# Attention and an expert layer in one kernel: where the preparation of w_out stands in the program

## The chip, the cores and the metric

The kernel runs on one core of a Trainium2 chip. The metric is device time in microseconds (us) of one execution. The core has five engines that run side by side and wait for one another by semaphores: TensorE (PE in the rows, with PEld for its weight loads), VectorE (DVE), ScalarE (ACT), GpSimd (POOL) and SyncE (SP), whose queue issues the DMAs here. Each engine takes its instructions strictly in the order in which the program lists them, so that an instruction that waits also holds back all that stand behind it on the same engine.

## The reference

```python
def _attn_ref(q, k, v):                      # 8 batches, 8 heads, 576 positions, 64 wide
    scores = scale * np.matmul(q, k.transpose(0, 1, 3, 2))
    mask = block_i >= block_j                # blocks of 64 positions
    scores = np.where(mask, scores, -1000000000.0)
    scores = scores - np.max(scores, axis=-1, keepdims=True)
    attn = np.exp(scores)
    attn = attn / (np.sum(attn, axis=-1, keepdims=True) + 1e-09)
    return np.matmul(attn, v)

def _moe_ref(x, w_in, w_out):                # 4608 tokens, 512 -> 2048 -> 512
    h = x @ w_in
    r = np.maximum(h, 0.0)
    return ((r * r) @ w_out)
```

The output of the attention, with the heads side by side, is the `x` of the second function. Everything is fp32 outside.

## The kernel before

**Attention** is worked in 40 passes, numbered 0 to 39. Passes 0 to 7 take the first 192 positions of batches 0 and 1, one pair of heads each; passes 8 to 15 take the other 384 positions of the same two batches; passes 16 to 39 take a whole pair of heads of batches 2 to 7. A pass is done in two or three groups of rows. For a group TensorE makes the scores (tile `ps`), VectorE the row maxima (`nmx`), ScalarE the exponentials with their sums (`sm`), VectorE the reciprocals (`rs`), and the probabilities (`p_rows`) are turned: in passes 8 to 11 by TensorE transposes (`pt`) that VectorE and ScalarE copy back, from pass 12 on by DMA transposes that SyncE issues (L480). Then TensorE multiplies by the values (`px`).

**The expert layer** is worked in 12 chunks of 384 tokens. A chunk's input (`xt`) is the normalized attention output as two fp16 parts. The hidden stage (`moe_in`) has 16 blocks of 12 matmuls (`ph`), each followed by ScalarE (`r`, `g`), GpSimd (`r*r`) and a subtraction (`g`, L680). The output stage (`moe_out`) has three accumulations of 48 matmuls (`po`), so a chunk has 192 + 144 = 336 matmuls. Chunk 0 holds what passes 0 to 7 give.

**The weights** come as fp32 in raw 64-bit blocks and are split into two fp16 parts on the core. `weight_scale(0)` and `weight_parts(0)` do it for w_in; `weight_scale(1)` and `weight_parts(1)` for w_out. For w_out each of the 16 blocks is loaded twice: once as `wa` for its maximum (VectorE, L245), once as `wb` for its parts: ScalarE `wt` (L283), three VectorE operations (L284, L287, L290), a ScalarE cast to `w2h` (L291), a GpSimd subtraction to `w2l` (L292). The scale of all parts needs the maxima of all 16 blocks; it goes through a transposition and a small matmul on TensorE (`pm_w`, L177 and L183). Both loads use the same ring of three buffers (`qk32`), which later holds the raw q and k of passes 16 on.

**What sets the order.** The Python program emits instructions in some order; that order is the priority. A scheduler then walks through them with a built-in timing and writes down for each engine the ready instruction of highest priority. The expert layer and the weights are generators, listed in `todo`; `fill(n)` advances them by n steps, and `pour` calls it between the groups of each pass (`FILL` gives the steps per pass). `first_moe` is the generator of chunk 0: a step is one block of the hidden stage or one block of w_in's parts; from the ninth block of the hidden stage on, each block is followed by one maximum of w_out, and when the hidden stage is through come the other maxima and then w_out's 16 blocks of parts, one a step. With 14 steps per pass, passes 8 to 11 take all of this in among their own work.

The constants `SC0`, `SCN`, `PTN` and `PT0` say where `first_moe` starts what; `WT`, `BP`, `BS`, `gate` and `behind` are switches for variants that are off.

Of the kernel before, what the change touches and what calls it, by code (L numbers as in the profile page):

```python
# [8 lines left out]
F32 = mybir.dt.float32  # L9
# [5 lines left out]
ALU = mybir.AluOpType  # L15
AX = mybir.AxisListType
PSUM = bass.MemoryType.PSUM

P = 128
# [5 lines left out]
NF = 16  # L25
# [6 lines left out]
A_X = 13  # L32
# [5 lines left out]

TLS = True
PRE = 0  # L40
SC0 = 8
SCN = 1
PTN = 3
PT0 = 16
G_POOL = 8
G_CK = 1
X_POOL = 1
QF = (6, 7)
WT = 1
IVN = 6  # L50
PT_MM = 8
EV = ((1, 1), (1, 0))
# [3 lines left out]
N_POOL = 0  # L56
N_HP = 2
NQ_CK = 1
BP = 99
BS = 99  # L60
NQ_POOL = 0
SQ_HP = 1
NG = 4
# [37 lines left out]
def attention_moe_kernel(ctx: ExitStack, tc: tile.TileContext, qkt, qk, vm, vt, w_in, w_out, out):  # L101
    nc = tc.nc
# [3 lines left out]
    p1 = ctx.enter_context(tc.tile_pool(name="p1", bufs=1))  # L106
# [98 lines left out]
        nc.sync.dma_start(raw, src[f])  # L205
        return words(raw)

    def behind(later, earlier):

        tc.add_manual_dep(  # L210
            later.ins,
            earlier.ins.name,
            mybir.DependencyInfo(mybir.DependencyClass.NoSync, mybir.DependencyReason.DATA),
            reason="order of use",
        )

    w1raw = []
    gate = {}

    wsc = [const.tile([P, n], F32, name=f"wsc{i}") for i, n in enumerate((NG, 1))]  # L220
    wm = const.tile([P, NG], F32, name="wm")
# [14 lines left out]
    def weight_scale(wi):  # L236

        tok, ng = ((tokA, NG), (tokB, 1))[wi]  # L240
        st = small.tile([P, NF], F32, tag="stw", name=f"stw_{wi}", bufs=1)
        n = NF // ng
        for f in range(NF):
            _, _, hf = load_w(w_out, f, f"wa{wi}_{f}") if wi else w1raw[f]
            i = nc.vector.tensor_reduce(st[:, f : f + 1], hf, axis=AX.X, op=ALU.max, apply_absolute_value=True)  # L245
            if wi == 0 and f >= BS and (1, 0) in gate:
                behind(i, gate[1, 0])
            if f % n == n - 1:
                q = f // n
                st1 = small.tile([P, 1], F32, tag="st1", name=f"st1_{wi}_{q}", bufs=1)  # L250
                nc.vector.reduce_max(st1, st[:, f + 1 - n : f + 1], axis=AX.X)
                m = pow2_of_max(st1, 1, f"w{wi}_{q}", 2.0**-27, wm[:, q : q + 1] if wi == 0 else None)
                s = wsc[wi][:, q : q + 1]
                nc.vector.tensor_scalar(
                    s.bitcast(I32), m.bitcast(I32), -1, (127 + W_TOP) << 23, op0=ALU.mult, op1=ALU.add
                )
            yield
        if wi == 0:
            m = small.tile([P, 1], F32, tag="m", name="m_w")
            nc.vector.reduce_max(m, wm, axis=AX.X)  # L260
        nc.vector.tensor_scalar(
            tok.bitcast(I32), m.bitcast(I32), 8, (127 - W_EXP) << 23, op0=ALU.mult, op1=ALU.add
        )
        if wi == 0:
            nc.vector.tensor_scalar(tokA, tokA, 2.0 ** (A_X + A_W - 1), None, op0=ALU.mult)
            inv = scale_of(m, 0, 1, "w")
            nc.vector.tensor_scalar(wm, wm, inv, None, op0=ALU.mult)
            nc.vector.tensor_tensor(wm, wm, wm, op=ALU.mult)
        else:
            nc.vector.tensor_scalar(tokB, tokB, tokA, None, op0=ALU.mult)  # L270
            nc.vector.tensor_scalar(wm, wm, wsc[1], None, op0=ALU.mult)

    def weight_parts(wi):

        wh, wl = ((w1h, w1l), (w2h, w2l))[wi]
        for f in range(NF):
            wlo, whi, hf = load_w(w_out, f, f"wb{wi}_{f}") if wi else w1raw[f]
            if WT:
                t = p1.tile([P, 512], F32, tag=("qs", "k1", "k2")[(wi + f) % 3], name=f"wt{wi}_{f}")
            else:  # L280
                t = p2.tile([P, 512], F32, tag="r", name=f"wt{wi}_{f}", bufs=3)
            q = f * NG // NF
            nc.scalar.activation(t, hf, AF.Copy, scale=(wm if wi else wsc[0])[:, q : q + 1])  # L283
            i = nc.vector.tensor_scalar(whi, whi, -(2**31), None, op0=ALU.bitwise_and)  # L284
            if wi == 0 and f >= BP and (1, 0) in gate:
                behind(i, gate[1, 0])
            nc.vector.scalar_tensor_tensor(  # L287
                whi, t.bitcast(I32), 3, whi, op0=ALU.logical_shift_left, op1=ALU.bitwise_or
            )
            nc.vector.scalar_tensor_tensor(whi, wlo, 29, whi, op0=ALU.logical_shift_right, op1=ALU.bitwise_or)  # L290
            nc.scalar.copy(wh[:, f], hf)  # L291
            nc.gpsimd.tensor_tensor(wl[:, f], hf, wh[:, f], op=ALU.subtract)  # L292
            yield
# [266 lines left out]
    def normalize(b, g):  # L560

        u = f"{b}_{g}"
        ck, o = place(b, g)
        w = D * TILES[g]
        if ck not in xts:
            slot = min(ck % 3, 1)
            xts[ck] = p1.tile([P, 2, NHP, CH], F16, tag=f"xt{slot}", name=f"xt_{ck}")
            ivs[ck] = small.tile([P, 3], F32, tag="iv", name=f"ivs_{ck}")
        x = x_of(b, g)
        early = ck < X_POOL  # L570
        nq = ps_x.tile([P, 512], F32, tag="x", name=f"nq_{u}")[:, :w]
        n = 3 * NHP // TILES[g]
        for a in range(0, NHP, n):
            sq = p1.tile([P, n, w], BF16, tag="sq", name=f"sq_{u}_{a}")
            if ck == 0 and SQ_HP:
                for hp in range(n):
                    nc.scalar.activation(sq[:, hp], x[:, a + hp], AF.Square)
            else:
                nc.scalar.activation(sq, x[:, a : a + n], AF.Square)
            k = n  # L580
            if ck >= NQ_CK:
                k = n // 2
                eng = nc.gpsimd if NQ_POOL else nc.vector
                eng.tensor_tensor(sq[:, 0:k], sq[:, 0:k], sq[:, k:n], op=ALU.add)  # L584
                if k > 1:
                    k = 1
                    eng.tensor_tensor(sq[:, 0:k], sq[:, 0:k], sq[:, k : 2 * k], op=ALU.add)
            for i in range(k):
                nc.tensor.matmul(nq, ones_bf, sq[:, i], start=(a + i == 0), stop=(a + n == NHP and i == k - 1))
        hb = p2.tile([P, CH], F32, tag="hb", name=f"hb_{u}")[:, :w]  # L590
        hi = hb.bitcast(I32)
        nc.vector.tensor_scalar(
            hi, nq.bitcast(I32), 1, EXPMASK, op0=ALU.logical_shift_right, op1=ALU.bitwise_and
        )
        gate[b, g] = nc.vector.tensor_scalar(hi, hi, -1, (190 + A_X) << 23, op0=ALU.mult, op1=ALU.add)  # L595
        xh, xl = xts[ck][:, 0, :, o : o + w], xts[ck][:, 1, :, o : o + w]
        if ck == 0 and b in N_DVE:
            for a in range(0, NHP, N_HP):
                hps = slice(a, a + N_HP)
                nc.vector.tensor_tensor(x[:, hps], x[:, hps], hb[:, None, :].to_broadcast([P, N_HP, w]), op=ALU.mult)  # L600
                (nc.scalar.copy if N_ACT else nc.vector.tensor_copy)(xh[:, hps], x[:, hps])
                (nc.gpsimd if N_POOL else nc.vector).tensor_tensor(xl[:, hps], x[:, hps], xh[:, hps], op=ALU.subtract)
            return ck, o, w, hb
        nc.gpsimd.tensor_tensor(x, x, hb[:, None, :].to_broadcast([P, NHP, w]), op=ALU.mult)  # L604
        (nc.scalar.copy if early else nc.vector.tensor_copy)(xh, x)  # L605
        nc.gpsimd.tensor_tensor(xl, x, xh, op=ALU.subtract)  # L606
        return ck, o, w, hb
# [22 lines left out]

    def first_moe(ck, firsts):

        scale, parts = weight_scale(1), weight_parts(1)
        hidden = moe_in(ck)
        n = 0
        while True:
            try:
                next(hidden)
            except StopIteration as e:
                gs = e.value  # L640
                break
            if n == IVN:
                for r in firsts:
                    inverses(*r)
            yield
            if next(parts0, 0) is None:
                yield
            for _ in range(SCN if n >= SC0 else 0):
                if next(scale, 0) is None:
                    yield  # L650
            if n == PT0:
                yield from scale
            for _ in range(PTN if n >= PT0 else 0):
                if next(parts, 0) is None:
                    yield
            n += 1
        for gen in (scale, parts):
            yield from gen
        yield from moe_out(ck, gs)

    def moe_in(ck):
# [116 lines left out]
    def emit(i0, i1):  # L778
        for i in range(i0, i1):
            one_pass(i, passes[i])  # L780
# [69 lines left out]
    todo.append(first_moe(0, firsts))  # L850
    front(passes[NT * NHP])
    pg = ctx.enter_context(tc.tile_pool(name="pg", bufs=16, reuse_waits="tile"))
    emit(NT * NHP, len(passes))
    while todo or waiting:
        fill(1)
# [32 lines left out]
```

## Time and profile before

| | us |
|---|---|
| median of 3 runs | 1152.78 (1150.38 to 1157.13) |
| the profiled execution | 1157.18 |
| its span, first to last instruction | 1155.4 |
| TensorE busy | 1035.3 (90%) |
| VectorE busy | 763.9 (66%) |
| ScalarE busy | 629.6 (54%) |
| GpSimd busy | 341.0 (30%) |

The busy time of TensorE is near to the span, so what the span has beyond it is the time in which TensorE waited. The table does not say where; the rows by stage below do. The mean granted clock over the span is 0.963 of the full one.

### The profile page before, as it was taken

What the parts mean: (1) busy time and instruction counts of PE and PEld (TensorE: products, weight loads), DVE (VectorE), ACT (ScalarE), POOL (GpSimd) and SP (SyncE); (2) the same over time, 40 slices, a digit from 0 to 9 for tenths busy, and PEclk for the clock granted to TensorE, in tenths of its full rate; (3) what the DMA queues carried; (4) which work ended last, traced back from release to release, by engine and by line L of the source; (5) the groups of instructions that cost most, each with busy time, mean ns of one, the idle gap of its engine ahead of it and who ended that gap; (6) DMA issues with size and microseconds to landing.
All of it is one profiled execution on the core that took longest, in us unless ns stands there. A gap on an engine that the chain in (4) does not pass through costs nothing. (4 is left out here: it accounts for less than half of the span.)

```text
span 1155.4 us, 18711 instructions
## 1 busy us (share of the span) xinstructions
PE 1035.3 (90%) x6836; PEld 541.6 (47%) x6836; DVE 763.9 (66%) x1783; ACT 629.6 (54%) x1492; POOL 341.0 (30%) x312
## 2 busy tenths in 40 slices
PE   6679777898989989899997999889889999999998
PEld 4234322354445445445544545445445545555453
DVE  6998789869778978868749857976896613212120
ACT  6586765557468548726737627726865723223140
POOL 2575145124112412422205302520340314312030
PEclk9799998899999999999999999989999999999999
DMA  8555177867687688855954657567848330000000
GB/s 282 194 186 194 56 193 188 198 140 140 144 165 156 114 191 164 155 115 114 186 120 84 141 111 138 119 140 148 170 80 169 48 78 20 10 19 1 28 1 28
DMA packets 337948, 142.25 MB, mean 123 GB/s; under 512 B 309696, under 2 KB 323008, under 8 KB 337856
## 3 DMA queue, kind: packets, MB, share of 16 engines
q1 hardware_dynamic: 337856, 141.06, 55.2%
q8 instruction: 53, 0.87, 0.3%
q14 instruction: 39, 0.32, 0.1%
HBM read 55.31 MB, written 9.44 MB: 56 GB/s over the span
## 5 line engine op out<-in xcount | busy, mean ns | idle before, releaser
L670 PE MATMUL ph<-xt,w1h 128*128 128x384 f16 x1536 | 381.2, 330 | 21.7 <-ACT r L676 10.4
L695 PE MATMUL po<-w2h,g 128*128 128x512 f16 x1152 | 359.7, 386 | 8.5 <-ACT w2h L291 8.5
L679 POOL TENSOR_TENSOR r<-r 128x384 f32<-128x384 f32 x192 | 178.6, 936 | 556.4 <-ACT g L678 520.3
L695 PEld LDWEIGHTS <-g 128*128 128x128 f16 x1728 | 166.3, 99 | 219.4 <-issue 34.1
L670 PE MATMUL ph<-xt,w1l 128*128 128x384 f16 x768 | 253.3, 330 | 0.0
L695 PE MATMUL po<-w2l,g 128*128 128x512 f16 x576 | 222.1, 386 | 4.2 <-POOL w2l L292 4.2
L670 PEld LDWEIGHTS <-w1h 128*128 128x128 f16 x1536 | 145.0, 99 | 129.6 <-issue 34.4
L452 ACT ACTIVATE p<-ps,nmx,es 128x320 f32<-128x320 f32 (+8 forms) x216 | 131.1, 616 | 135.9 <-DVE nmx L449 111.4
L676 ACT ACTIVATE r<-ph 128x384 f32<-128x384 f32 x192 | 93.2, 491 | 160.3 <-PE ph L670 147.9
L680 DVE TENSOR_TENSOR g<-r,g 128x384 f16<-128x384 f32 x184 | 113.7, 623 | 86.3 <-POOL r L679 86.2
L476 DVE SCALAR_TENSOR_TENSOR p_rows<-p,rs,p_rows 128x320 f16<-128x320 f32 (+8 forms) x240 | 143.5, 632 | 18.6 <-ACT p_rows L475 18.3
L475 ACT ACTIVATE p_rows<-p,rs 128x320 f16<-128x320 f32 (+8 forms) x240 | 120.3, 569 | 47.1 <-DVE rs L461 23.1
L446 DVE TENSOR_REDUCE nmx<-ps 128x1 f32<-128x192 f32 (+8 forms) x288 | 124.6, 479 | 23.5 <-PE ps L422 14.8
L678 ACT ACTIVATE g<-r 128x384 f16<-128x384 f32 x192 | 99.4, 525 | 4.0 <-POOL w1l L292 0.8
L670 PEld LDWEIGHTS <-w1l 128*128 128x128 f16 x768 | 75.8, 99 | 51.2 <-issue 2.2
L422 PE MATMUL ps<-kT,qT 128*64 128x64 f16 (+6 forms) x960 | 84.7, 297 | 10.6 <-DMA qT<-qs 5.8
L534 PE MATMUL px<-p_turned,v 128*64 128x384 f16 (+5 forms) x1168 | 79.3, 282 | 14.5 <-DMA p_turned<-p_rows 10.1
L702 DVE TENSOR_SCALAR ob<-po,uv 128x512 f32<-128x512 f32 x36 | 28.9, 805 | 95.7 <-PE po L695 95.7
L534 PEld LDWEIGHTS <-v 128*64 128x64 f16 x1128 | 54.7, 115 | 48.1 <-issue 22.1
L604 POOL TENSOR_TENSOR x<-x,hb 128x768 f32<-128x768 f32 (+1 forms) x16 | 44.6, 2785 | 94.9 <-DVE hb L595 92.8
L422 PEld LDWEIGHTS <-qT 128*64 128x64 f16 x960 | 45.9, 111 | 50.5 <-issue 31.7
L606 POOL TENSOR_TENSOR xt<-x,xt 128x768 f16<-128x768 f32 (+1 forms) x16 | 51.7, 3229 | 30.9 <-DVE xt L605 24.3
(129 smaller groups left out, 965.3 us busy)
## 6 DMA issues: line engine op xcount, KB each, us to landing
qk<-in_qk SPq DMA_DIRECT2D x24, 576.0 KB, 4.5
wa<-in_w_out SPq DMA_DIRECT2D x16, 512.0 KB, 4.3
wb<-in_w_out SPq DMA_DIRECT2D x16, 512.0 KB, 4.4
out<-ob SPq DMA_DIRECT2D x32, 256.0 KB, 2.1
vraw<-in_vm SPq DMA_DIRECT2D x30, 256.0 KB, 3.5
w1raw<-in_w_in SPq DMA_DIRECT2D x8, 512.0 KB, 6.6
kf<-in_qkt SPq DMA_DIRECT2D x8, 288.0 KB, 3.6
w2h<-in_w_in SPq DMA_DIRECT2D x4, 512.0 KB, 10.9
```

Source lines behind the costliest of these rows:

```text
L422: nc.tensor.matmul(ps[hs, o].rearrange("p (n d) -> p n d", d=D), t["qT"][:, j, hs], t["kT"][:, z, c0:c1, hs], start=(z == 0), stop=(z == 1),)
L446: nc.vector.tensor_reduce(nmx[:, i : i + 1], ps[:, off : off + w], axis=AX.X, op=ALU.max, negate=True)
L452: nc.scalar.activation(p32[:, off : off + w], ps[:, off : off + w], AF.Exp, bias=nmx[:, i : i + 1], scale=es, accum_out=sm[:, i : i + 1],)
L475: nc.scalar.activation(hi, p32[:, off : off + w], AF.Copy, scale=rs[:, i : i + 1])
L476: nc.vector.scalar_tensor_tensor(lo, p32[:, off : off + w], rs[:, i : i + 1], hi, op0=ALU.mult, op1=ALU.subtract)
L534: nc.tensor.matmul(px[hs, D * a :].rearrange("p (j d) -> p j d", d=D), lhs, rhs, start=(c == 0 and pi == 0), stop=(c == NCH[g] - 1 and (pi ...
L670: nc.tensor.matmul(ph[:, :CH], w[:, f, P * cc : P * cc + P], xt[:, z, cc, :], start=(i == 0), stop=(i == 11))
L676: nc.scalar.activation(r, ph[:, :CH], AF.Relu, scale=c)
L678: nc.scalar.activation(g[:, 0], r, AF.Square)
L679: nc.gpsimd.tensor_tensor(r, r, r, op=ALU.mult)
L680: (nc.gpsimd if f < G_POOL and ck < G_CK else nc.vector).tensor_tensor(g[:, 1], r, g[:, 0], op=ALU.subtract)
L695: nc.tensor.matmul(po, gs[f][:, z, P * t : P * t + P], w[:, f, :], start=(i == 0), stop=(i == 3 * NF - 1))
```

## The change

`first_moe` no longer counts steps: in every step of the hidden stage it advances w_in's parts and w_out's maxima by one block each, and when the hidden stage is through it emits all 16 blocks of w_out's parts. The main program calls `fill(2 * NF)`, 32 steps, before the first of passes 8 to 39 is emitted. So the hidden stage of chunk 0, the maxima and the parts of w_out all have priority over passes 8 on; only the output stage of chunk 0 is left for `pour`. The switches that were off are removed; the instructions are the same.

```diff
@@ first_moe
-        scale, parts = weight_scale(1), weight_parts(1)
-        hidden = moe_in(ck)
+        hidden, scale = moe_in(ck), weight_scale(1)
         n = 0
         while True:
             try:
                 next(hidden)
...
             if n == IVN:
                 for r in firsts:
                     inverses(*r)
+            next(parts0, 0)
+            next(scale, 0)
             yield
-            if next(parts0, 0) is None:
-                yield
-            for _ in range(SCN if n >= SC0 else 0):
-                if next(scale, 0) is None:
-                    yield
-            if n == PT0:
-                yield from scale
-            for _ in range(PTN if n >= PT0 else 0):
-                if next(parts, 0) is None:
-                    yield
             n += 1
-        for gen in (scale, parts):
-            yield from gen
+        for _ in scale:
+            pass
+        for _ in weight_parts(1):
+            yield
         yield from moe_out(ck, gs)
@@ main program
     front(passes[NT * NHP])
     pg = ctx.enter_context(tc.tile_pool(name="pg", bufs=16, reuse_waits="tile"))
+
+    fill(2 * NF)
     emit(NT * NHP, len(passes))
```

In the program's rows the first number of a tile's name is left out and a running number stands at its end: `ps_0_0_4_2524` are scores of head pair 0 in a pass that starts at row block 0 (so one of passes 16 on), group of row block 4; `ph_4` is the fifth block of a hidden stage; `wb_0` the first raw block of w_out. The lines differ by the removed code: L284, L287, L290 of before are L262, L263, L266 of the change, L205 is L198, L670 is L640, L422 is L398.

VectorE where the parts of w_out begin, before:

```order
L284 TENSOR_SCALAR wb_0_1399<-wb_0_1399 128x512
L446 TENSOR_REDUCE nmx_1_3_8_1871<-ps_1_3_8_1869 128x1 x2
L287 SCALAR_TENSOR_TENSOR wb_0_1399<-wt_0_1401,wb_0_1399 128x512
L284 TENSOR_SCALAR wb_1_1408<-wb_1_1408 128x512
L509 COPY p_turned<-pt_1458 128x4x128
L284 TENSOR_SCALAR wb_2_1417<-wb_2_1417 128x512
L449 TENSOR_SCALAR nmx_1_3_8_1871<-nmx_1_3_8_1871 128x2
L476 SCALAR_TENSOR_TENSOR p_rows<-p_1_0_3_8_1702,rs_0_3_8_1705,p_rows 128x576
L290 SCALAR_TENSOR_TENSOR wb_0_1399<-wb_0_1399 128x512
L287 SCALAR_TENSOR_TENSOR wb_1_1408<-wt_1_1410,wb_1_1408 128x512
```

and in the change:

```order
L262 TENSOR_SCALAR wb_0_1071<-wb_0_1071 128x512
L262 TENSOR_SCALAR wb_1_1080<-wb_1_1080 128x512
L263 SCALAR_TENSOR_TENSOR wb_0_1071<-wt_0_1073,wb_0_1071 128x512
L263 SCALAR_TENSOR_TENSOR wb_1_1080<-wt_1_1082,wb_1_1080 128x512
L262 TENSOR_SCALAR wb_2_1089<-wb_2_1089 128x512
L266 SCALAR_TENSOR_TENSOR wb_0_1071<-wb_0_1071 128x512
L266 SCALAR_TENSOR_TENSOR wb_1_1080<-wb_1_1080 128x512
L263 SCALAR_TENSOR_TENSOR wb_2_1089<-wt_2_1091,wb_2_1089 128x512
L436 TENSOR_SCALAR sm_1_3_4_1556<-sm_1_3_4_1556 128x2
L266 SCALAR_TENSOR_TENSOR wb_2_1089<-wb_2_1089 128x512
L437 RECIPROCAL rs_1_3_4_1557<-sm_1_3_4_1556 128x2
L436 TENSOR_SCALAR sm_2_3_8_1606<-sm_2_3_8_1606 128x2
```

Before, the parts of w_out stand among the row maxima of pass 13 (`nmx_1_3_8`), the copies of turned probabilities and the split of pass 12's probabilities (`p_rows`, L476). In the change they stand among the sums of passes 9 and 10 (`sm_1_3_4`, `sm_2_3_8`), and the split of pass 12 comes behind all 16 blocks.

SyncE where w_out's raw blocks are loaded, before:

```order
L205 DMA wb_3_1473<-in_w_out 128x512
L205 DMA wb_4_1482<-in_w_out 128x512
L205 DMA wb_5_1510<-in_w_out 128x512
L334 DMA qz_3_3_2062<-in_qkt 64x384 x2
L335 DMA kf_3_3_2063<-in_qkt 128x576
L205 DMA wb_6_1519<-in_w_out 128x512
L480 DMA_TRANSPOSE p_turned<-p_rows 128x30x128
L205 DMA wb_7_1557<-in_w_out 128x512
L205 DMA wb_8_1566<-in_w_out 128x512
L480 DMA_TRANSPOSE p_turned<-p_rows 128x30x128
L205 DMA wb_9_1575<-in_w_out 128x512
```

and in the change:

```order
L198 DMA wb_3_1098<-in_w_out 128x512
L198 DMA wb_4_1107<-in_w_out 128x512
L198 DMA wb_5_1116<-in_w_out 128x512
L323 DMA vraw_80<-in_vm 128x2x256
L325 DMA vraw_80<-in_vt 64x2x64
L198 DMA wb_6_1125<-in_w_out 128x512
L310 DMA qz_0_3_1694<-in_qkt 64x384 x2
L311 DMA kf_0_3_1695<-in_qkt 128x576
L198 DMA wb_7_1134<-in_w_out 128x512
L198 DMA wb_8_1143<-in_w_out 128x512
L198 DMA wb_9_1152<-in_w_out 128x512
L310 DMA qz_1_3_1825<-in_qkt 64x384 x2
```

Before, DMA transposes of the probabilities stand between the loads of `wb`. In the change none does; the loads of q, k and values for passes 12 and 13 (`qz_0_3`, `kf_0_3`, `qz_1_3`, `kf_1_3`, `vraw`) stand there instead, behind the loads of the blocks before them.

TensorE where the scores of pass 16 begin, before:

```order
L670 LDWEIGHTS w1h
L670 MATMUL ph_4_2351<-xt_1922,w1h 128x384
L670 LDWEIGHTS w1l
L670 MATMUL ph_4_2351<-xt_1922,w1l 128x384
L422 LDWEIGHTS qT_0_0_2343
L422 MATMUL ps_0_0_4_2524<-kT_0_0_2344,qT_0_0_2343 64x320
```

and in the change:

```order
L640 LDWEIGHTS w1h
L640 MATMUL ph_13_2640<-xt_1990,w1h 128x384
L640 LDWEIGHTS w1l
L640 MATMUL ph_13_2640<-xt_1990,w1l 128x384
L398 LDWEIGHTS qT_0_0_2419
L398 MATMUL ps_0_0_4_2600<-kT_0_0_2420,qT_0_0_2419 64x320
```

Before, five blocks of chunk 1's hidden stage (`ph_0` to `ph_4`) stand ahead of these scores; in the change fourteen (`ph_0` to `ph_13`). Everything else that TensorE has ahead of them, but for two small matmuls of pass 17, is the same.

## Rows read from the trace of the kernel before

**Rows 1.** Busy time by stage; columns: stretch, its length, each engine, clock, DMA

```profile
0.00:50.00 50.00, 29.68 (x229) 18.88 (x230) 36.30 (x123) 29.59 (x94) 18.34 (x36) 0.80 0.85 275
50.00:100.00 50.00, 38.07 (x239) 20.43 (x239) 49.96 (x98) 37.40 (x82) 37.07 (x34) 1.00 0.51 169
100.00:136.00 36.00, 33.15 (x208) 17.11 (x206) 24.31 (x73) 26.63 (x68) 9.40 (x14) 1.00 0.36 108
136.00:210.00 74.00, 50.28 (x242) 19.04 (x240) 66.09 (x140) 41.24 (x79) 33.42 (x27) 0.83 0.68 176
210.00:230.00 20.00, 20.00 (x108) 9.03 (x105) 15.87 (x34) 11.97 (x29) 1.13 (x2) 0.93 0.88 196
230.00:330.00 100.00, 89.20 (x641) 47.26 (x640) 74.54 (x167) 55.94 (x133) 22.68 (x18) 0.98 0.74 149
330.00:900.00 570.00, 526.05 (x3782) 278.89 (x3780) 435.31 (x1038) 352.95 (x862) 152.74 (x118) 0.97 0.69 138
900.00:1156.00 256.00, 248.89 (x1402) 130.93 (x1400) 61.49 (x116) 73.90 (x150) 66.20 (x67) 1.00 0.09 23
```

**Rows 2.** What TensorE waited for, 50 to 230 us (total, times, longest)

```profile
PE po L695 <- ACT w2h L291: 8.5, 7, 2.2
...
PE po L695 <- POOL w2l L292: 4.2, 5, 1.4
```

**Rows 3.** VectorE in time order: the end of the maxima of w_out

```profile
104.10 0.16 DVE L251 TENSOR_REDUCE st<-stw 128x1 f32<-128x16 f32 x1
```

**Rows 4.** TensorE in time order (start, length), at five places

```profile
130.92 0.27 PE L177 MATMUL pm_w<-ident,st 128*1 128x128 f32 x1
...
229.34 0.49 PE L670 MATMUL ph<-xt,w1h 128*128 128x384 f16 x2
...
242.39 0.74 PE L422 MATMUL ps<-kT,qT 128*64 128x320 f16 x10
...
323.11 0.49 PE L670 MATMUL ph<-xt,w1h 128*128 128x384 f16 x2
...
424.05 0.49 PE L670 MATMUL ph<-xt,w1h 128*128 128x384 f16 x2
```

**Rows 5.** Instructions on the raw blocks wb: min/median/max ns, first to last start

```profile
L283 ACT ACTIVATE wt<-wb,wm x16: 743/770/818, 136.0 to 204.2; 128x512 f32<-128x512 f32 x16
...
L284 DVE TENSOR_SCALAR wb<-wb x16: 405/420/1335, 136.8 to 206.6; 128x512 int32<-128x512 int32 x16
...
L287 DVE SCALAR_TENSOR_TENSOR wb<-wt,wb x16: 670/683/3775, 138.5 to 207.6; 128x512 int32<-128x512 int32 x16
...
L290 DVE SCALAR_TENSOR_TENSOR wb<-wb x16: 669/686/1523, 141.2 to 208.3; 128x512 int32<-128x512 int32 x16
...
L292 POOL TENSOR_TENSOR w2l<-wb,w2h x16: 1142/1270/2126, 142.6 to 210.0; 128x512 f16<-128x512 f32 x16
```

**Rows 6.** The page, DMA issues: loads of wb (us to landing last)

```profile
wb<-in_w_out SPq DMA_DIRECT2D x16, 512.0 KB, 4.4
```

**Rows 7.** The queue of SyncE in time order (start, length), two entries

```profile
143.81 5.92 SPq L205 DMA_DIRECT2D wb<-in_w_out  x3
...
157.89 6.11 SPq L480 DMA_TRANSPOSE p_turned<-p_rows  x1
```

**Rows 8.** Chain that ended last: one hidden stage with nothing between

```profile
1026.35 31.20 PE ph L670 x192
```

**Rows 9.** VectorE groups by form (busy us, mean ns, idle before)

```profile
L680 DVE TENSOR_TENSOR g<-r,g 128x384 f16<-128x384 f32 x184 | 113.7, 623 | 86.3 <-POOL r L679 86.2
...
L384 DVE SCALAR_TENSOR_TENSOR k<-qk,s,k 128x576 f16<-128x576 f32 x24 | 19.5, 810 | 5.4 <-ACT k L382 5.4
...
L387 DVE SCALAR_TENSOR_TENSOR qs<-qk,s,qs 128x576 f16<-128x576 f32 x24 | 24.7, 1028 | 0.0
```

**Rows 10.** GpSimd in time order: the last step of two chunk inputs

```profile
288.75 3.33 POOL L606 TENSOR_TENSOR xt<-x,xt 128x1536 f16<-128x1536 f32 x1 [3.82 <-DVE xt L605]
...
403.61 4.58 POOL L606 TENSOR_TENSOR xt<-x,xt 128x1536 f16<-128x1536 f32 x1 [4.14 <-DVE xt L605]
```

More of the change, by code (lines that the diff above doesn't have):

```diff
@@ L40 @@
 PRE = 0
[L41 to L44, printed above, removed]
 G_POOL = 8
@@ L48 @@
 QF = (6, 7)
-WT = 1
 IVN = 6
@@ L58 @@
 NQ_CK = 1
-BP = 99
-BS = 99
 NQ_POOL = 0
@@ L206, in load_w @@
         return words(raw)
[L208 to L215, printed above, removed]
     w1raw = []
-    gate = {}
     wsc = [const.tile([P, n], F32, name=f"wsc{i}") for i, n in enumerate((NG, 1))]
@@ L244, in weight_scale @@
             _, _, hf = load_w(w_out, f, f"wa{wi}_{f}") if wi else w1raw[f]
-            i = nc.vector.tensor_reduce(st[:, f : f + 1], hf, axis=AX.X, op=ALU.max, apply_absolute_value=True)
-            if wi == 0 and f >= BS and (1, 0) in gate:
-                behind(i, gate[1, 0])
+            nc.vector.tensor_reduce(st[:, f : f + 1], hf, axis=AX.X, op=ALU.max, apply_absolute_value=True)
             if f % n == n - 1:
@@ L277, in weight_parts @@
             wlo, whi, hf = load_w(w_out, f, f"wb{wi}_{f}") if wi else w1raw[f]
[L278 to L281, printed above, removed]
+            t = p1.tile([P, 512], F32, tag=("qs", "k1", "k2")[(wi + f) % 3], name=f"wt{wi}_{f}")
             q = f * NG // NF
             nc.scalar.activation(t, hf, AF.Copy, scale=(wm if wi else wsc[0])[:, q : q + 1])
-            i = nc.vector.tensor_scalar(whi, whi, -(2**31), None, op0=ALU.bitwise_and)
-            if wi == 0 and f >= BP and (1, 0) in gate:
-                behind(i, gate[1, 0])
+            nc.vector.tensor_scalar(whi, whi, -(2**31), None, op0=ALU.bitwise_and)
             nc.vector.scalar_tensor_tensor(
@@ L594, in normalize @@
         )
-        gate[b, g] = nc.vector.tensor_scalar(hi, hi, -1, (190 + A_X) << 23, op0=ALU.mult, op1=ALU.add)
+        nc.vector.tensor_scalar(hi, hi, -1, (190 + A_X) << 23, op0=ALU.mult, op1=ALU.add)
         xh, xl = xts[ck][:, 0, :, o : o + w], xts[ck][:, 1, :, o : o + w]
```

## The prediction

> **What bounds the kernel now.** I read the busy time by stage first, then what TensorE waits for in the worst stage, then that stage's weights, engine by engine.
>
> By stage [rows 1], TensorE is short of its stretch by 11.9 us from 50 to 100, by 2.9 from 100 to 136, by 23.7 from 136 to 210, by nothing from 210 to 230. From 230 on it works 89 to 97% of the time, so the rest of the kernel is TensorE's, and a wait taken out early should come off the end if the same work is then further on. VectorE is the reverse: full from 50 to 100 (49.96 of 50), idle for 11.7 us from 100 to 136, nearly full again from 136 to 210 (66.1 of 74). The granted clock is 0.83 in that last stage and 1.00 in the two before it.
>
> The stage from 136 to 210 is w_out's parts: their first ScalarE step starts at 136.0, the last GpSimd step at 210.0 [rows 5]. TensorE waits there for exactly these, 8.5 us for the casts and 4.2 for the subtractions [rows 2]. But nothing of w_out's own made them start so late. The last of the maxima is reduced at 104.1 [rows 3], and TensorE transposes it only at 130.9 [rows 4], because in its order that small matmul stands behind scores and transposes of passes 10 to 12. For about 27 us, while VectorE has its idle time, work that VectorE must do later lies still.
>
> **The change, part by part.** No instruction is added or dropped; all of it is order.
>
> *The maxima.* In VectorE's new order they lie between the same neighbours as before, among w_in's parts in the stage where VectorE is full. I cost that at nothing: what hides it is that stage's own VectorE work, the same in sum; if the cover were gone, it would show as maxima that end later than 104.
>
> *The scale.* Its transposition now stands between the blocks 13 and 14 of chunk 0's hidden stage instead of behind attention. TensorE will wait there for the maxima, with two blocks queued behind it and the output stage behind those. Before, chunk 0's blocks wait for w_in's parts in the same stretch, so part of this wait replaces others. Its cost lies between 0 and the stage's whole present wait, 11.9 us; since VectorE, which is full there, has the same work ahead of it, I take 0 net.
>
> *The parts.* They start some 27 us earlier and run into VectorE's idle time instead of the full stage. Per block VectorE needs 0.42 + 0.68 + 0.69 = 1.79 us (medians), 28.6 for 16 [rows 5]. The three-buffer ring sets a floor of its own: from the first ScalarE step, 136.0, to the next load, 143.8 [rows 7], and 4.4 to land it [rows 6], a turn took 12.2 us for three blocks, so 65 us for 16 at that pace, against 75 measured (136.0 to 210.0 and 1.3 for the last). The difference is near to what SyncE's queue spent on transposes between the loads: one of them occupies it for 6.1 us [rows 7]. The change has none between the loads. What it has instead are loads for passes 12 to 15 that wait for older scores, with later raw blocks behind them on the same queue. A start 27 us earlier and 0 to 10 us less length: the parts can end 27 to 37 us earlier.
>
> *What that moves.* This is not the gain, since attention moves back in exchange. The cleanest place to weigh both is the first scores of pass 16, at 242.4 before [rows 4]. From there on both orders are alike in kind, and ahead of it the orders hold the same work but for this: on TensorE the change has 9 more blocks of chunk 1, 108 matmuls; on VectorE 8 more subtractions `g` and the preparation of pass 17. One matmul of the hidden stage takes 31.20 / 192 = 0.1625 us [rows 8], so TensorE is 17.6 us of work further. The VectorE work is 8 x 0.62 = 5.0, then 0.81 + 1.03 = 1.8, and nine small operations, none longer than the 0.42 of a 512-column one, for which I take 0.2 each, 1.8: 8.6 us [rows 9].
>
> If VectorE idles as long as before up to that place, pass 16's scores come 8.6 us later, at 251.0, with 17.6 us more done: 17.6 - 8.6 = 9.0 us gained. VectorE's idle time is the unknown. All of the 11.7 us of 100 to 136 filled would make the gain 20.7. Idle time added by new waits lowers it without a floor in the rows; the nearest measure is what VectorE idles in the two stages after 136, 7.9 + 4.1 = 12.0 us, and adding as much once more makes it 9.0 - 12.0 = -3.0. I take no change in idle time, because the two ends lie about equally far.
>
> *From there to the end.* At the last values of pass 19 the change is still 36 matmuls ahead, 5.9 us; the other 72 have been given back to attention, which is no loss while TensorE is the bound. Work that runs ahead can run dry: the input of chunk 2 is ready at 292.1 [rows 10] and its first matmul starts at 323.1 [rows 4], 31 us of slack; that of the next chunk is ready at 408.2 and used from 424.1, 15.9 us. A lead of 5.9 to 17.6 us uses much of that and not all. I cost this at nothing; if the cover is gone, each us beyond the slack is a us of wait.
>
> **Sum.** The profiled execution took 1157.2 us, its span 1155.4 and 1.8 around it; 1157.2 - 9.0 = 1148.2. It lies 4.4 us above the median of the runs shown, 1152.8, so for a median I expect 1152.8 - 9.0 = 1143.8.
>
> **Rivals.**
> *Given back.* VectorE and the chains of attention set the pace after 230 (VectorE works 74.5 of the next 100 us), so attention that is 8.6 us late stays late, and the matmuls done ahead only turn into waits. For it: TensorE still waits 11% of 230 to 330. Against it: 97% from 900 on. It leaves between 0 and the 5.9 us of lead at pass 19: about 1150.
> *The parts lock with attention.* Place: TensorE between `po` of chunk 0 and scores of passes 10 to 13, which stand in turns. A VectorE maximum waits for scores, these for `po` of an older block, that for the parts of it, and these are behind the maximum or, through SyncE, behind a load that waits for scores. Before, a block took 75.3 / 16 = 4.7 us; with a third of a ring turn more of waiting, 4.1 us, for every third block, it takes 6.1, and the stage gets 22 us longer. 1152.8 - 9.0 + 22 = 1166. It decides from where pass 16's scores come later than 242.4 + 17.6 = 260.0. For it: the long waits for w_out's parts [rows 2], with less room here. Against it: two or three blocks lie between the links.
> *Two engines on one memory port.* One of the VectorE steps takes 0.69 us as a rule and 1.52 at worst [rows 5]; in the change they and GpSimd's subtractions fill the same stretch. If one step of each block is stretched so, 16 x 0.84 = 13.4 us, and 1152.8 - 9.0 + 13.4 = 1157. The Trainium skill, GPSIMD Engine Reference, Specifications, says that GpSimd shares its memory interfaces with VectorE and that operations with two inputs in memory contend. The trace agrees that such steps are stretched at times, by 0.84 us; no row says how often in the change.
>
> **How the numbers follow.** Within 0.5%, 5.8 us, a measurement of this kernel tells nothing from no change. The forecast, with up to 20.7 us of gain, gets 0.53 and is faster. Given back, 0.24, is the same. The lock, 0.18, is slower. The port, 0.05, is split between same and slower. So faster 0.53, same 0.26, slower 0.21. The forecast alone holds 1132 to 1147. The range goes from 1131 to 1161: the full idle time filled at one end, half of the lock's price and the port's at the other; beyond it I leave the worse half of the lock and a little below.
>
> **What would show it.** Right: w_out's parts start near 110 and end before 185; no stage around them has a clock near 0.83; chunk 1's hidden stage starts between 190 and 215 instead of 229.3; pass 16's scores come between 240 and 255; TensorE's total wait falls by about the gain, its busy time hardly. Wrong: scores of pass 16 after 260, parts that last more than 75 us, or a new wait of TensorE ahead of chunk 2 or 3. If the early stages gain as said and the end does not, the step that failed is the one from pass 19 to the end.

## The result, and the profile after

The kernel became slower by 0.4%: 1160.3 us, median of 20 runs (1156.7 to 1164.3), against 1156.3 in 20 runs of the kernel before beside it; the ratio is 1.004, with an interval of 1.0024 to 1.0057. 1143.8 was forecast. Of the 16.5 us between forecast and measurement 3.5 lie in the base, since three runs had given 1152.8 for the kernel before and 20 give 1156.3; the rest is the effect, 9.0 us of gain forecast and 4.0 us of loss measured. The profiled execution took 1162.8 us, 5.6 more than that of before.

Busy time by stage of the changed kernel; columns as in [rows 1]:

```profile
0.00:50.00 50.00, 28.98 (x226) 18.13 (x228) 35.69 (x123) 29.16 (x94) 17.82 (x36) 0.80 0.82 275
50.00:100.00 50.00, 35.34 (x202) 17.28 (x199) 49.95 (x93) 31.99 (x70) 35.31 (x33) 0.97 0.46 154
100.00:136.00 36.00, 28.80 (x162) 15.64 (x162) 27.61 (x63) 24.16 (x52) 15.23 (x17) 0.95 0.49 162
136.00:210.00 74.00, 59.91 (x332) 28.31 (x333) 51.62 (x125) 43.43 (x92) 23.26 (x25) 0.93 0.56 155
210.00:230.00 20.00, 17.72 (x113) 8.34 (x111) 15.91 (x40) 12.92 (x32) 5.87 (x4) 0.91 0.60 114
230.00:330.00 100.00, 86.82 (x624) 45.45 (x621) 74.28 (x181) 58.03 (x141) 21.09 (x16) 0.93 0.74 145
330.00:900.00 570.00, 517.54 (x3722) 274.63 (x3720) 429.14 (x1030) 347.13 (x846) 147.30 (x115) 0.97 0.70 138
```

The stage of w_out's parts, 136 to 210, is better, as meant: TensorE lacks 14.1 us there instead of 23.7 [rows 1], and its clock is 0.93 instead of 0.83. But it lacks 14.7 from 50 to 100 (11.9 before), 7.2 from 100 to 136 (2.9) and 2.3 from 210 to 230 (0). From 50 to 230 that makes 38.2 us of waiting against 38.5. What one stage won, its neighbours lost. So with the clock: those three neighbours ran at 0.97, 0.95 and 0.91, before at 1.00, 1.00 and 0.93.

What TensorE waited for from 50 to 230 (total, times, longest); the last two rows are the kernel before's, for the first and third:

```profile
PE ps L387 <- ACT p L428: 12.3, 7, 3.3
PE px L510 <- DMA p_turned<-p_rows: 7.1, 1, 7.1
PE ph L640 <- ACT r L646: 6.8, 7, 1.5
...
PE po L665 <- ACT w2h L267: 1.2, 1, 1.2
PE po L665 <- POOL w2l L268: 1.0, 2, 0.8
```

```profile
PE ps L411 <- ACT p L452: 5.3, 6, 1.4
...
PE ph L670 <- ACT r L676: 2.4, 2, 1.7
```

The waits for w_out's parts are nearly gone, 2.2 us where there were 12.7 [rows 2]. In their place TensorE waits for ScalarE behind the hidden stage (`ph`, 4.4 us more), which now runs with little attention between its blocks, and for attention (`ps`, 7.0 us more, and `px`, 7.1 us in one wait), which now runs with little expert work between its steps.

TensorE in time order, at places of [rows 4]: the scale's two matmuls, chunk 1, the scores of pass 16:

```profile
106.05 0.27 PE L170 MATMUL pm_w<-ident,st 128*1 128x128 f32 x1
...
110.70 0.17 PE L176 MATMUL pm_w<-dg_w,ones_bf 1*128 1x1 bf16 x1
...
212.83 0.49 PE L640 MATMUL ph<-xt,w1h 128*128 128x384 f16 x2 [1.97 <-DVE xt L581]
...
262.95 0.54 PE L398 MATMUL ps<-kT,qT 128*64 128x320 f16 x4
```

The raw blocks `wb` (min, median, max ns; first and last start):

```profile
L261 ACT ACTIVATE wt<-wb,wm x16: 755/766/782, 113.2 to 170.9; 128x512 f32<-128x512 f32 x16
...
L263 DVE SCALAR_TENSOR_TENSOR wb<-wt,wb x16: 676/692/707, 115.0 to 172.2; 128x512 int32<-128x512 int32 x16
L266 DVE SCALAR_TENSOR_TENSOR wb<-wb x16: 683/790/1545, 116.5 to 173.5; 128x512 int32<-128x512 int32 x16
...
L268 POOL TENSOR_TENSOR w2l<-wb,w2h x16: 1147/1189/1688, 119.9 to 175.2; 128x512 f16<-128x512 f32 x16
```

The scale is transposed 25 us earlier, the parts take 63 us instead of 75 [rows 5] and end 34 us earlier, chunk 1 starts 16.5 us earlier. And yet the scores of pass 16 come 20.6 us later than before, where 8.6 was forecast. The stretch from the start to those scores, in the kernel before and, below it, in the changed one:

```profile
0.00:242.39 242.39, 183.29 (x1103) 91.15 (x1104) 201.44 (x480) 154.08 (x363) 102.43 (x114) 0.90 0.65 183
```

```profile
0.00:262.95 262.95, 198.68 (x1214) 103.19 (x1214) 203.74 (x496) 162.36 (x381) 106.26 (x122) 0.91 0.60 172
```

VectorE (the third pair) worked 2.3 us more and idled 59.2 us instead of 40.9. The rows by stage say where: from 100 to 136, the stage that the parts were to fill, its idle time only fell from 11.7 to 8.4 us, and from 136 to 210 it rose from 7.9 to 22.4. A place where it stands still, in time order, first VectorE, then ScalarE, then TensorE:

```profile
185.49 0.82 DVE L340 TENSOR_REDUCE st<-vraw 128x1 f32<-128x640 f32 x1 [3.50 <-DMA vraw<-in_vt]
189.24 0.81 DVE L672 TENSOR_SCALAR ob<-po,uv 128x512 f32<-128x512 f32 x1 [2.93 <-PE po L665]
...
189.46 1.07 ACT L451 ACTIVATE p_rows<-p,rs 128x384 f16<-128x384 f32 x2 [8.39 <-PE pt L483]
...
178.68 0.38 PE L665 MATMUL po<-w2h,g 128*128 128x512 f16 x1 [0.56 <-DVE ob L672]
...
189.04 0.82 PE L483 MATMUL pt<-ident,p_rows 128*128 128x128 f32 x6
...
207.66 3.20 PE L510 MATMUL px<-p_turned,v 128*64 128x384 f16 x30 [7.12 <-DMA p_turned<-p_rows]
```

From 178.7 to 189.0 TensorE does chunk 0's third output accumulation, 48 matmuls in a row. Pass 11's last turning (`pt`) stands behind it, and `p_rows` of pass 12 can't be written before that turning, so ScalarE waits 8.4 us and VectorE does only one reduction, between idle stretches of 3.5 and 2.9 us. Then TensorE has no more of chunk 0, chunk 1's input isn't there until 212.8, and the wait comes back to it: 7.1 us for pass 12's turned probabilities. The first DMA transpose of `p_turned` starts at 195.7, before at 157.9 [rows 7].

### The profile page after: what moved, and what is told of

Its sections match the earlier page's. It is cut to its first block, busy times and chain, and to the rows that moved or that the text cites. A ratio compares the mean times of both kernels' runs of the same rounds, so it can differ in the third digit from the quotient of the medians.

```text
span 1161.0 us, 18694 instructions
## 1 busy us (share of the span) xinstructions
PE 1030.0 (89%) x6836; PEld 542.3 (47%) x6836; DVE 757.5 (65%) x1783; ACT 628.8 (54%) x1492; POOL 334.1 (29%) x312
## 5 line engine op out<-in xcount | busy, mean ns | idle before, releaser
L640 PE MATMUL ph<-xt,w1h 128*128 128x384 f16 x1536 | 386.9, 334 | 22.5 <-ACT r L646 13.6
L665 PE MATMUL po<-w2h,g 128*128 128x512 f16 x1152 | 354.1, 381 | 5.4 <-DVE g L650 3.7
L665 PEld LDWEIGHTS <-g 128*128 128x128 f16 x1728 | 166.6, 98 | 204.4 <-issue 11.9
L640 PE MATMUL ph<-xt,w1l 128*128 128x384 f16 x768 | 255.5, 333 | 0.0
L665 PE MATMUL po<-w2l,g 128*128 128x512 f16 x576 | 218.8, 380 | 1.0 <-POOL w2l L268 1.0
L640 PEld LDWEIGHTS <-w1h 128*128 128x128 f16 x1536 | 145.9, 99 | 135.8 <-issue 42.0
L452 DVE SCALAR_TENSOR_TENSOR p_rows<-p,rs,p_rows 128x576 f16<-128x576 f32 (+8 forms) x240 | 146.3, 643 | 35.7 <-ACT p_rows L451 35.0
L451 ACT ACTIVATE p_rows<-p,rs 128x576 f16<-128x576 f32 (+8 forms) x240 | 120.8, 571 | 60.8 <-DVE rs L437 21.0
L422 DVE TENSOR_REDUCE nmx<-ps 128x1 f32<-128x192 f32 (+8 forms) x288 | 123.8, 477 | 21.4 <-PE ps L387 12.6
L640 PEld LDWEIGHTS <-w1l 128*128 128x128 f16 x768 | 76.5, 100 | 54.0 <-issue 6.0
L510 PE MATMUL px<-p_turned,v 128*64 128x384 f16 (+5 forms) x1168 | 75.6, 278 | 28.6 <-DMA p_turned<-p_rows 26.4
L398 PE MATMUL ps<-kT,qT 128*64 128x64 f16 (+6 forms) x960 | 82.4, 295 | 16.5 <-DMA qT<-qs 9.3
L398 PEld LDWEIGHTS <-qT 128*64 128x64 f16 x960 | 45.0, 111 | 60.2 <-issue 36.6
L387 PE MATMUL ps<-kf,qz 128*64 128x512 f32 (+5 forms) x224 | 47.6, 545 | 12.7 <-ACT p L428 12.6
```

The lines of the kernel that those rows point to most:

```text
L398: nc.tensor.matmul(ps[hs, o].rearrange("p (n d) -> p n d", d=D), t["qT"][:, j, hs], t["kT"][:, z, c0:c1, hs], start=(z == 0), stop=(z == 1),)
L422: nc.vector.tensor_reduce(nmx[:, i : i + 1], ps[:, off : off + w], axis=AX.X, op=ALU.max, negate=True)
L451: nc.scalar.activation(hi, p32[:, off : off + w], AF.Copy, scale=rs[:, i : i + 1])
L452: nc.vector.scalar_tensor_tensor(lo, p32[:, off : off + w], rs[:, i : i + 1], hi, op0=ALU.mult, op1=ALU.subtract)
L510: nc.tensor.matmul(px[hs, D * a :].rearrange("p (j d) -> p j d", d=D), lhs, rhs, start=(c == 0 and pi == 0), stop=(c == NCH[g] - 1 and (pi ...
L640: nc.tensor.matmul(ph[:, :CH], w[:, f, P * cc : P * cc + P], xt[:, z, cc, :], start=(i == 0), stop=(i == 11))
```

## The experiments

The measure is the one of the prediction: when the scores of pass 16 come, and how many blocks of chunk 1 (12 matmuls, 1.95 us each) TensorE has done by then beyond the kernel before. *Net* is the work done ahead minus the lateness; *end* the gain in the profiled execution's span against 1155.4. Both columns rest on one execution each, and 20 executions of the kernel before spread over 10.8 us, so differences of 2 or 3 us in them are not clear of that scatter. The ratio is to runs of the kernel before in the same session and is the firmest column.

| run | blocks ahead | scores | net | end | median | ratio to before, interval |
|---|---|---|---|---|---|---|
| before | 0 | 242.4 | 0 | 0 | 1156.3 | |
| the change | 9 | 263.0 | -3.0 | -5.6 | 1160.3 | 1.0040 (1.0024 to 1.0057) |
| e1 | 3 | 243.8 | 4.5 | -5.0 | 1165.6 | 1.0093 (1.0064 to 1.0122) |
| e2 | 3 | 252.0 | -3.8 | -1.5 | 1154.5 | 1.0000 (0.9983 to 1.0017) |
| e3 | -5 | 252.2 | -19 | -30.6 | 1188.8 | 1.0288 (1.0260 to 1.0316) |
| e4 | 6 | 249.4 | 4.7 | 10.3 | 1149.0 | 0.9942 (0.9922 to 0.9961) |
| e5 | 9 | 256.6 | 3.4 | 3.4 | 1155.3 | 0.9996 (0.9978 to 1.0014) |
| e6 | 5 | 251.9 | 0.2 | -10.0 | 1167.3 | 1.0099 (1.0070 to 1.0127) |
| e7 | 6 | 250.7 | 3.4 | -0.6 | 1158.0 | 1.0014 (0.9995 to 1.0033) |
| e8 | 5 | 249.1 | 3.0 | -9.5 | 1167.3 | 1.0095 (1.0070 to 1.0121) |
| e9 | 4 | 249.4 | 0.8 | -0.6 | 1154.7 | 1.0001 (0.9985 to 1.0017) |
| e10 | 6 | 249.5 | 4.6 | -2.9 | 1161.7 | 1.0055 (1.0035 to 1.0075) |
| e11 | 6 | 250.5 | 3.6 | 13.9 | 1141.9 | 0.9883 (0.9862 to 0.9903) |
| e12 | 6 | 254.2 | -0.1 | 6.0 | 1150.9 | 0.9968 (0.9953 to 0.9983) |
| e13 | 5 | 243.0 | 9.2 | 7.7 | 1151.1 | 0.9962 (0.9945 to 0.9980) |

**Where chunk 0's output stands (e1 to e3).** `behind` sets only the order on an engine; `gate` holds the last matmul of a pass's turning or values. In e1 the generator rests for 56 steps before the third accumulation:

```diff
-        yield from moe_out(ck, gs)
+        n = 0
+        for _ in moe_out(ck, gs):
+            n += 1
+            if n == 8:
+                for _ in range(64 - 8):
+                    yield
+            yield
@@ moe_out
+                    if ck == 0 and t == 2 and i == 0:
+                        behind(m, gate["px", 12, 1])
```

Expected of e1: 

> Chunk 0's third output accumulation (po_2, 48 matmuls, 10.3 us) stands behind the values of pass 12 in TensorE's order instead of ahead of pass 11's last turning transpositions; nothing else is changed on purpose. Theory A (that block alone keeps pass 12 back): the first DMA transposes of p_turned start about 10 us earlier than 195.7, near 185, the scores of pass 16 between 250 and 256, and the time is 1150 to 1155. Theory B (the whole attention of passes 8 to 11 is late, behind chunk 0's hidden stage and the output matmuls that go at the parts' pace): the transposes start 3 to 10 us earlier, the time falls by 1 to 4 us, to 1156 to 1159. Theory C (the loss arises after pass 19): 1159 to 1162, whatever the transposes do.

The transposes started at 185.5, as A said, and the scores came at 243.8, earlier than A said; the time was 5 us worse than the change's and outside all three ranges. Chunk 1's steps stand behind the resting generator, so e1 moved them too; e9 mends that.

In e2 and e3 all three accumulations are held, for 56 and 64 steps; the first two are put behind `gate["pt", 11]` and `gate["px", 12, 1]`, and the third follows them.

Expected of e2: 

> All three output accumulations of chunk 0 stand behind the last turning transpositions of pass 11 in TensorE's order; maxima, scale and parts of w_out are where the change has them. Theory A: no better than the run with the third one alone moved, 1150 to 1155. Theory B: pass 11's turning no longer waits for the parts, so the first transposes of p_turned start at 160 to 175 and the scores of pass 16 at 240 to 250; chunk 1 starts later than 212.8 by up to 10; time 1148 to 1153. Theory C: 1159 to 1162.

Expected of e3: 

> All three output accumulations of chunk 0 stand behind the values of pass 12. Theory A: 1150 to 1155, like the run with the third one alone. Theory B: first transposes of p_turned at 155 to 170, scores of pass 16 at 230 to 245, while chunk 1 starts at 225 to 232, as in the kernel before; what TensorE does ahead of those scores shrinks with it, so the time is 1148 to 1155. Theory C: 1159 to 1162.

Theory B's remedy fails. The transposes started at 183.2 and 179.0, not at 155 to 175: that is only 2.3 and 6.5 us earlier than in e1, so attention of passes 8 to 11 is hardly faster when the other output matmuls step aside too. e3's 1188.8 us lie far outside every range: TensorE is left without work for 39.7 us from 100 to 220 (120 less the 80.35 of its row; 23.6 in the change), and chunk 1, held back with the rest, starts at 251.8:

```profile
100.00:220.00 120.00, 80.35 (x442) 38.78 (x442) 90.57 (x209) 73.14 (x160) 38.85 (x42) 0.83 0.57 153
```

e2 is 0.4% below the change, with scores no better placed (net -3.8 against -3.0), so what it gained arose behind them; its time lies below C's range, 1159 to 1162. That the change's own loss arises early, against C, is shown by e5, e9 and e13 below: there the early order gets better, and so does the end.

**How much goes ahead of pass 8 (e4 to e7).** e4 takes out the change's last line; e5 halves it; e6 and e7 are e4 with another first entry of `FILL`:

```diff
-    fill(2 * NF)          # e4, e6, e7: nothing
+    fill(NF)              # e5
...
-FILL = (14, 5, 7, 7, 10, 10, 8, 7)
+FILL = (9, 5, 7, 7, 10, 10, 8, 7)     # e6;  20 in e7
```

Expected of e4: 

> The change without its line that gives hidden stage, maxima and parts to the scheduler ahead of pass 8's attention: the order of the steps alone (one maximum and one part per hidden block, then the parts, then the output) is poured in between passes 8 to 11. Theory A: the third accumulation stands within the values of pass 12 here, so about the kernel before, 1152 to 1157. Theory B: attention of passes 8 to 11 is less far back, first transposes of p_turned 170 to 185, time 1152 to 1157. Theory C: between the two kernels, 1156 to 1160.

Expected of e5: 

> Only chunk 0's hidden stage and the maxima are given to the scheduler ahead of pass 8's attention; w_out's parts are poured in with pass 8. Theory D (what costs is that attention of passes 8 to 11 is put behind chunk 0's work): between the run without the line and the change, 1152 to 1158, first transposes of p_turned 180 to 195. Theory P (it is the 16 parts ahead that hold attention back): like the run without the line, 1147 to 1152, first transposes near 172. Theory E (after the early stages any other order moves the time by chance by some us, whatever is ahead): anywhere from 1150 to 1165, without a link to the transposes.

Expected of e6: 

> The order of the steps alone, without the line, poured in between passes 8 to 11 at 9 steps a pass instead of 14. Theory D: w_out's parts end later (about 205 instead of 200), attention is 0 to 5 us earlier; 1147 to 1153, near the run with 14. Theory E: 1145 to 1160.

Expected of e7: 

> The same with 20 steps a pass instead of 14: a half-way house to the change. Theory D: first transposes of p_turned between 172 and 196, chunk 1 starts 213 to 217, time between the two, 1150 to 1157. Theory E: 1145 to 1160, without a link.

e4 beats both kernels, with 1149.0 us below the ranges of all three theories: at 14 steps a pass the new order of the steps is a gain, and the line that puts 32 of them ahead of pass 8 is what loses it. e7, with more, is slower, as D has it, 1 us above D's range. But e6, with still less ahead, is 18 us slower than e4 and outside both ranges, so D doesn't hold alone. P is wrong as well, since in e5 the transposes start at 192.4, nearly as late as in the change.

e5 is the most telling. Its order differs from the change's in few places, all ahead of pass 16's scores: turning transpositions of passes 9 to 11 stand, most of them, a few places further ahead among `po` of chunk 0, their copies ahead of a step on w_out's parts, and some steps of the last passes before pass 16 have changed places with blocks of chunk 1. From the scores of pass 16 on both orders are alike, row for row, on all engines. VectorE idled 52.0 us up to the scores (256.59 less 204.57), 7.2 less than in the change:

```profile
0.00:256.59 256.59, 200.40 (x1213) 105.10 (x1213) 204.57 (x496) 161.62 (x381) 107.18 (x122) 0.91 0.61 176
```

The net at the scores is 6.4 us better, the time 0.44% (5.1 us). So much of the change's time hangs on these early places. The first transposes of `p_turned` come 3.3 us earlier, so about half of the 6.4 us arises ahead of them and half behind; which of the places carries how much was not tried.

**Who goes first after that (e8).** The change, with `FILL = (14, 3, ...)`.

Expected of e8: 

> The change, with 3 steps of chunk 1 poured in with each of passes 12 to 15 instead of 5, so that their attention stands ahead of more of chunk 1. Theory F (the lead of TensorE is lost because the inputs of chunks 2 and 3 come too late, with no slack): inputs of chunks 2 and 3 ready 5 to 10 us earlier than 309.2 and 419.2, time 1150 to 1156. Theory D (the loss is made ahead of pass 12 and cannot be won back by who goes first later): 1157 to 1162.

Theory F is refuted. The inputs of chunks 2 and 3 came 17.9 and 14.8 us earlier than in the change, at 291.3 and 404.4, both with over 25 us to spare, and the kernel was 7 us slower, which is above D's range, too.

**The third accumulation alone (e9), and in e4's order (e10).** The rest of chunk 0's output is now put into the list when pass 12's values have been emitted, and chunk 1 is poured as in the change:

```diff
-        yield from moe_out(ck, gs)
+        out0 = moe_out(ck, gs)
+        for _ in range(8):
+            next(out0)
+            yield
+        gate["rest"] = out0
@@ finish
         values(t, g)
+        if (t["i"], g) == (12, 1):
+            todo.insert(0, gate["rest"])
@@ moe_out
+                    if ck == 0 and t == 2 and i == 0:
+                        behind(m, gate["px", 12, 1])
```

Expected of e9: 

> The run with the third accumulation behind pass 12's values held back chunk 1's pouring as well; here that accumulation alone is moved, and chunk 1 is poured in as in the change. Theory N (the loss is made ahead of the scores of pass 16, where pass 11's turning stands behind that block): scores of pass 16 near 246 with 49 matmuls (8.0 us) more ahead of them than in the kernel before, so 3 to 5 us ahead of it there, and as much at the end: 1150 to 1154. Theory E (any other order behind pass 12 shifts the time by up to 10 us): 1145 to 1166.

Expected of e10: 

> The order of the steps alone, without the line, and chunk 0's third accumulation behind all of pass 12's values, where it stood between them. Theory N: the values of pass 12 are done 7 to 10 us earlier, and where their chain was waited for the gain is up to 5 us: 1143 to 1149. Theory E: 1143 to 1160.

e9 takes back 0.39%, 4.5 us. ScalarE's wait for the turning is gone (L462 is L451 of the change):

```profile
180.74 0.83 ACT L386 ACTIVATE v<-vraw,s 128x640 f16<-128x640 f32 x1 [0.81 <-DVE s L184]
181.63 1.07 ACT L462 ACTIVATE p_rows<-p,rs 128x384 f16<-128x384 f32 x2
```

VectorE idled 49.1 us up to the scores (249.42 less 200.33):

```profile
0.00:249.42 249.42, 189.95 (x1154) 99.15 (x1154) 200.33 (x480) 156.63 (x369) 100.82 (x118) 0.90 0.60 177
```

That is theory N's answer in kind: the net rises from -3.0 to 0.8. In size it is less than N said, scores at 249.4 instead of 246 and a net of 0.8 instead of 3 to 5, and the time is 0.7 us above N's range. In e10 the same edit made e4's order 1.1% slower, 1161.7 us, which is above E's range as well as N's. Nothing was lost up to the scores there, 4.6 against 4.7; everything was lost behind them, so N does not reach that far.

**Both early losses together (e13).** e9's edit and `fill(NF)`.

Expected of e13: 

> Hidden stage and maxima ahead, the parts poured in with pass 8, and chunk 0's third accumulation moved behind pass 12's values. Theory N with two separate losses (attention's turning behind the parts' steps, and that block ahead of pass 11's turning): the two gains of some 5 us each add up, 1147 to 1152. Rival (one hole ahead of the scores of pass 16 that either edit fills): like either alone, 1153 to 1158. Theory E: anywhere from 1145 to 1166.

The ratio is 0.78% below the change's; the two edits alone gave 0.44% and 0.39%. At the scores the nets rose by 6.4 and 3.8 us alone and by 12.2 together. Both add up, as two separate losses would. The stretch up to the scores:

```profile
0.00:242.97 242.97, 187.78 (x1163) 96.93 (x1163) 202.27 (x485) 158.04 (x373) 102.34 (x119) 0.93 0.63 183
```

VectorE idles 40.7 us, as long as before (40.9), and the net at the scores is 9.2 us. With VectorE's idle time as the prediction had it, a gain like the prediction's 9.0 us is there. That the two numbers are so near is luck, since the terms differ: 5 blocks ahead and 0.6 us late here, 9 blocks and 8.6 us in the prediction. The clock up to the scores was higher as well, 0.93 against 0.91 in the change, and its share was not separated. At the end the profiled execution keeps 7.7 us of the 9.2, and 12 runs keep 0.38%, 4.4 us.

**The rate of pouring in e4's order (e11, e12).** 16 and 12 steps a pass.

Expected of e11: 

> The order of the steps alone, without the line, poured in at 16 steps a pass. Theory G (attention and chunk 0 hide each other's waits best where both last equally long, a smooth optimum between 9 and 20 steps a pass): 1148 to 1154. Theory E: 1145 to 1165, not between the runs with 14 and 20.

Expected of e12: 

> The same at 12 steps a pass. Theory G: between the runs with 9 and 14, 1150 to 1160. Theory E: anywhere from 1145 to 1170.

With 9, 12, 14, 16 and 20 steps the medians are 1167.3, 1150.9, 1149.0, 1141.9 and 1158.0: one peak near 16, the shape that G has, with steep sides; e12 lies in G's range, e11 well below it and below E's. G's reason, that both last equally long, was not tested, and five points can't tell a smooth curve from E's scatter: e6 and e7 show how near the bad orders lie. The Trainium skill, Perfetto Trace Analysis, Optimization Strategy, says that interleaving stretches with different limits can pay beside work within each. This curve agrees at 16 steps a pass, 1.6% faster than hidden stage and parts ahead as a block, and not at 9 a pass, 0.6% slower than the block. e11 is the best kernel of the study, 1.2% below the one before. Its net at the scores is no better than e4's; its gain comes behind them. TensorE's stretch from 220 to 420, in e4 and then in e11:

```profile
220.00:420.00 200.00, 179.63 (x1342) 96.00 (x1341) 155.35 (x380) 127.61 (x310) 49.20 (x39) 0.98 0.79 153
```

```profile
220.00:420.00 200.00, 185.38 (x1373) 97.98 (x1371) 158.64 (x390) 131.71 (x320) 51.26 (x40) 0.98 0.80 160
```

It waits 14.6 us there instead of 20.4. In e11's order most of the last scores of pass 16 stand some 50 matmuls further ahead; which of its moved rows makes the difference was not tried.

## Why the prediction was wrong

**Right, step by step.** The maxima cost next to nothing: the last of them is reduced at 105.5, against 104.1 [rows 3]. The parts started at 113 (near 110 was said), ended 34 us earlier (27 to 37), at 176.7, and no stage around them had a clock near 0.83. Chunk 1 started at 212.8 (190 to 215). TensorE had the 9 blocks ahead, 17.6 us.

**The scale, taken as 0 of 0 to 11.9.** What TensorE waited for from 50 to 136, in the kernel before and, below, in the changed one:

```profile
PE ps L411 <- ACT p L452: 3.2, 4, 1.4
PE ph L670 <- ACT r L676: 2.4, 2, 1.7
...
PE pm_w L183 <- DVE dg_w L182: 1.6, 1, 1.6
```

```profile
PE ps L387 <- ACT p L428: 9.4, 4, 3.3
PE ph L640 <- ACT r L646: 6.8, 7, 1.5
PE pm_w L176 <- DVE dg_w L175: 2.5, 1, 2.5
```

The wait on the scale itself (`pm_w` for `dg_w`) grew by only 0.9 us, so the 0 was near. But TensorE lacks 7.1 us more than before in this stretch: blocks of the hidden stage wait 4.4 us more for ScalarE and scores 6.2 us more, while other waits got shorter. I looked at the wait that the step would add and not at what had been standing between these blocks.

**The step that failed: "If VectorE idles as long as before up to that place".** It idled 18.3 us more. The other term was off as well, the other way: VectorE's busy time grew by 2.3 us instead of the 8.6 that I summed. The kinds of instruction that I had added up took 8.8 us more, near to what I had said, but others took 6.5 us less (the longest of L287, now L263, took 0.71 us, before 3.78 [rows 5]). So the lateness is 2.3 + 18.3 = 20.6, and the net 17.6 - 20.6 = -3.0. That it is the lower end that I had written down is luck: there 12.0 us of idle time stood beside 8.6 us of work. In e13, where the idle time is that of before, the net is a gain of 9.2 us. The choice of the middle, "because the two ends lie about equally far", was the mistake: the new order already held `po` of chunk 0 ahead of pass 11's turning, and pass 12's split of probabilities behind all 16 blocks, each of them a reason for more idle time.

**From the scores to the end, costed at nothing.** It cost 2.6 us in one execution of each kernel, which is not clear of the scatter between executions. I set the lead against the slack of chunks 2 and 3, 31 and 15.9 us. But their slack shrinks by lead and lateness together. GpSimd's end of their inputs, in the changed kernel:

```profile
305.63 3.61 POOL L582 TENSOR_TENSOR xt<-x,xt 128x1536 f16<-128x1536 f32 x1 [3.73 <-DVE xt L581]
...
413.60 5.55 POOL L582 TENSOR_TENSOR xt<-x,xt 128x1536 f16<-128x1536 f32 x1 [4.30 <-DVE xt L581]
```

Chunk 2 starts at 312.9, 3.6 us behind its input; chunk 3 at 417.0, while GpSimd is still writing the second part of its own, to 419.2. The missing slack is not shown to cost anything. e5 has no more of it, with the input of chunk 2 ready at 302.6 and used from 306.2 and that of chunk 3 ready at 412.0 and used from 411.4, and lost nothing behind the scores; e8 gave the slack back and was slower:

```profile
299.02 3.60 POOL L582 TENSOR_TENSOR xt<-x,xt 128x1536 f16<-128x1536 f32 x1 [3.74 <-DVE xt L581]
...
406.44 5.54 POOL L582 TENSOR_TENSOR xt<-x,xt 128x1536 f16<-128x1536 f32 x1 [4.30 <-DVE xt L581]
```

**The rivals.** *The parts lock with attention* had its condition fulfilled, scores later than 260.0, and its side was the right one. Its mechanism wasn't: the parts' stage got 12 us shorter, not 22 longer, and TensorE waited 2.2 us for parts. What stood in turns was `po` and the turning of pass 11. *Given back* would be the 2.6 us behind the scores, which are not clear of the scatter. *One memory port*: the stretched step's median is 0.79 us instead of 0.69; its 16 blocks took 15.1 us together instead of 12.1, 3.0 more and not 13.4. Eight of the 16 took over 0.85 us, before two, each of them beside a subtraction of GpSimd's. The Trainium skill, GPSIMD Engine Reference, Specifications, has VectorE and GpSimd contend in VectorE's steps with two inputs in memory; the trace agrees in kind, with a small size here.

**What stays open.** Behind pass 16's scores the runs whose pouring is the change's (the change, e5, e9, e13) lose 0 to 2.6 us by their profiled executions and 0.9 to 4.8 us by their ratios. Against the change, e5, e9 and e13 rose by 6.4, 3.8 and 12.2 us at the scores and by 5.1, 4.5 and 9.0 us in the ratio, so for these the reading at the scores carries over, if not in full. Those with another pouring or a held generator gain or lose up to 12.5 us there (e11 +10.3, e8 -12.5), more than the whole effect of the change, and for them the net at the scores says little of the end. No experiment took that apart.

## What to carry to other kernels

Here work that is independent of a chain was worth most between the chain's steps; pulled ahead as a block it ended its own wait (12.7 us to 2.2) and uncovered two others, its own between its blocks and the chain's between its steps. So when a change fills an engine's hole, ask what used to lie between the instructions that now stand alone, and read in the new order what is queued behind the block on TensorE: here 48 matmuls ahead of one turning cost 4.5 us of 1160. And slack shrinks by lead and lateness together: 31 us became 3.6, though no run shows that this cost time.

## What the runs showed that was not expected

A few rows decide: e5 and the change are alike on all engines from pass 16 on and differ by 0.44%. And the sign of an edit depended on what surrounded it: the third accumulation moved behind pass 12's values gained 0.39% in the change's order and cost 1.1% in e4's. Such a gain has to be run again in a neighbouring order before it is counted there.
